# Attention decode on one core: the final wait moved behind the closing barrier, first loads ahead of the opening branch, last head scaled on VectorE

## The chip, the cores and the metric

The kernel runs on one core of one Trainium2 chip. The metric is device microseconds of that core, lower is better. "Span" below is the time from the first to the last instruction that the profiler recorded; it is shorter than the device time.

## The reference, cut to what matters

```python
B, H, Sq, Sk, D = 1, 16, 1, 8192, 256           # bf16
scores = einsum("bhqd,bhkd->bhqk", q, k) * D**-0.5
p = softmax(scores, axis=-1)
return einsum("bhqk,bhkd->bhqd", p, v)
```

One query row per head meets 8192 keys and values. K and V are 67 MB each and every byte is used once, so this is mainly a matter of loading 134 MB.

## The kernel before

The kernel records all operations of each engine in a plan, resolves semaphores, and then emits the plan into one block with a body per engine. In the program the block opens with a branch of each engine to its own body and closes with a branch to a common end, where a barrier of all five engines stands: each engine drains and reports ("gather"), GpSimd collects the reports and lets all go ("release"). An opening barrier of the same kind, which guards some constants (four memsets of GpSimd, 0.236 to 0.425 us; release at 0.597), stands ahead of the block.

Loads of K and V go out on SyncE, 2 MB each (some of V in smaller parts, the last two of 256 KB), four buffers of each kind:

```python
plan.op("act", lambda e: e.dma_start(q16[:, :], q[0, :, 0, :]), "q", dma=(s_q, 16))
for kind, h, x in items:                 # k and v halves in order of use
    ...
        plan.op("sp", lambda e, ...: e.dma_start(b[:, at*D:(at+wd)*D], cols(t, h, c+at, c+at+wd)),
                f"{kind}{n}.{i}", waits, dma=(s, used[id(s)]))
```

VectorE computes three quarters of the scores and TensorE the rest; TensorE multiplies the exponentials with V; ScalarE scales each head's sum by the reciprocal of its denominator:

```python
def final(h):
    s = sl(h)
    act(lambda e: e.activation(out=o[0:1, h*D:(h+1)*D], in_=acc[s][0:1, 0:D],
                               func=ACT.Copy, scale=recip[0:1, s:s+1]),
        f"fin{h}", [f"vfree{2*h+1}", f"rc{h}"], ksem("fin", h))
```

The end, on ScalarE's queue; the first 15 heads have been sent out earlier as "out0":

```python
final(H - 1)
plan.op("act", lambda e: e.dma_start(out[0, H-1, 0:1, :], o[0:1, (H-1)*D:H*D]),
        "out1", [f"fin{H-1}"], dma=(s_o[1], 16))
plan.op("act", lambda e: e.nop(), None, ["out0", "out1"])   # wait for both landings
...
with nc.Block() as block:
    ...                                   # plan.emit for each engine
```

## Time and profile before

| what | value | where it is read |
|---|---|---|
| device time | 323.13 us, median of 6 (322.97 to 323.22) | the timed runs |
| span | 321.3 us, so 1.8 us of the device time lie outside it | first line of the page |
| DMA engines busy | over 90% in 38 of 40 slices, 418 GB/s | slice rows of the page and its DMA line |
| first K load issued | 0.72 us | timeline |
| last matmuls, scaling, output's issue | 317.31, 319.26, 319.75 us | timeline |

Lines of the profile page. In the slice rows, each digit is the busy share of one fortieth of the span in tenths; the group line has count, then busy us and mean ns of one, then the idle time before and its releaser.

```profile
span 321.3 us, 6420 instructions
...
PE 221.4 (69%) x2166; PEld 155.5 (48%) x2166; DVE 275.2 (86%) x1586; ACT 94.1 (29%) x185; POOL 1.9 (1%) x12
DMA  7999999999999999999999999999999999999994
q1 hardware_dynamic: 10080, 134.22, 98.5%
L618 ACT ACTIVATE o<-acc,recip 1x256 bf16<-1x256 f32 x16 | 7.5, 466 | 74.1 <-PE acc L604 74.1
```

The load queue holds the DMA engines for 98.5% of the span: the kernel is one load stream with a head and a tail that nothing covers. The opening, in the timeline (start us, length us, engine, line, operation):

```profile
0.72 0.85 SPq L318 DMA_DIRECT2D Kb<-in_k_dram  x2
0.73 0.40 ACTq L300 DMA_DIRECT2D q<-in_q_dram  x1
```

The end, in the chain of waits (start us, length us, what) and then in the timeline:

```profile
304.67 12.60 DMA Vb<-in_v_dram
317.27 0.04 issue
317.31 1.92 PE acc L604 x16
319.24 0.02 issue
319.26 0.47 ACT o L618
```

```profile
319.26 0.47 ACT L618 ACTIVATE o<-acc,recip 1x256 bf16<-1x256 f32 x1 [7.36 <-PE acc L604]
319.75 0.24 ACTq L686 DMA_DIRECT2D out_dram<-o  x1
```

The timeline leaves semaphore instructions out. They are in the trace's records, and the last 1.3 us consist of them (start us, length us, engine, record; the words at the end are added):

```
319.754 0.238 Scalar  DMA_DIRECT2D     issue of out1
320.857 0.017 Scalar  EVENT_SEMAPHORE  out1's landing is seen
320.912 0.038 Scalar  COMPARE_BRANCH   closing branch; it carries the wait for out0
321.077 0.008 Scalar  DRAIN            ScalarE reports to the closing barrier
321.118 0.017 GpSimd  EVENT_SEMAPHORE  all have reported
321.196 0.017 GpSimd  EVENT_SEMAPHORE  release
321.238 0.017 Sync    EVENT_SEMAPHORE  released
321.242 0.017 Scalar  EVENT_SEMAPHORE  released
321.249 0.021 Vector  EVENT_SEMAPHORE  released
321.249 0.051 Tensor  EVENT_SEMAPHORE  released: end of the span, 321.300
```

From the landing to the end of the span 321.300 - 320.857 = 0.44 us pass with branch, drain and barrier.

### The profile page before, as it was taken

To read this page: it belongs to the slowest core of one execution; us is meant where nothing else is said; L and a number is where in the kernel's file an instruction comes from. 1 tells how busy PE (TensorE), PEld (TensorE's weight loads), DVE (VectorE), ACT (ScalarE), POOL (GpSimd) and SP (SyncE) were. 2 spreads that over 40 slices of the span, in tenths; PEclk is the share of its full clock that TensorE was granted. 3 is DMA by queue.
4 is the path that set the end of the run, shared out by engine and by line. 5 is a ranking of instruction groups with operands and counts; after the bars stand their busy time and mean duration, and the time that the engine had idled before them with its cause. 6 is when DMAs were issued, how large, how long until landed. Compare 5 with 4: busy or idle time off the path is not lost.

```text
span 321.3 us, 6420 instructions
## 1 busy us (share of the span) xinstructions
PE 221.4 (69%) x2166; PEld 155.5 (48%) x2166; DVE 275.2 (86%) x1586; ACT 94.1 (29%) x185; POOL 1.9 (1%) x12
## 2 busy tenths in 40 slices
PE   1645238687676858785977666687567876486896
PEld 0524126565454635563655454455444645354574
DVE  0899999999999999999998988889988889888600
ACT  3453222414233242422141242213322213232010
POOL 2000000000000000000000000000000000000000
PEclk9999999979797987997697898959898779779799
DMA  7999999999999999999999999999999999999994
GB/s 306 434 430 423 428 426 426 426 434 422 425 430 426 430 428 428 430 426 428 430 428 426 428 430 428 426 428 430 427 426 428 430 425 428 432 426 428 416 417 171
DMA packets 10126, 134.36 MB, mean 418 GB/s; under 512 B 1138, under 2 KB 1155, under 8 KB 1796
## 3 DMA queue, kind: packets, MB, share of 16 engines
q1 hardware_dynamic: 10080, 134.22, 98.5%
q8 instruction: 5, 0.08, 0.1%
q14 instruction: 5, 0.04, 0.0%
q10 hardware_dynamic: 36, 0.02, 0.0%
HBM read 134.23 MB, written 0.01 MB: 418 GB/s over the span
## 4 chain that ended last, share of the span: by engine, by line
DVE 46%; DMA 46%; PE 4%; issue 2%; SPq 0%; DVEq 0%; ACT 0%
DVE prod L359 44%; DMA Vb<-in_v_dram 25%; DMA Kb<-in_k_dram 21%; PE acc L604 4%; DVE S L359 2%; DVE g L331 0%; SPq L318 0%; DVE recip L340 0%; DVEq L150 0%; DVE m L378 0%; ACT o L618 0%; DVEq L147 0%; DVEq L144 0%
## 5 line engine op out<-in xcount | busy, mean ns | idle before, releaser
L359 DVE CUSTOM_DVE_ANT_0 prod<-Kb,qbc 128x256 bf16<-128x256 bf16 x768 | 269.1, 411 | 27.2 <-DMA Kb<-in_k_dram 24.7
L604 PE MATMUL acc<-Vb,E 128*1 128x256 bf16 x1024 | 146.0, 312 | 9.8 <-DMA Vb<-in_v_dram 9.8
L604 PEld LDWEIGHTS acc<-Vb,E 128*1 128x1 bf16 x1024 | 95.4, 95 | 52.7 <-DMA Vb<-in_v_dram 11.0
L499 ACT ACTIVATE KT<-tp 128x1024 bf16<-128x1024 bf16 x64 | 62.0, 1021 | 113.1 <-PE tp L490 113.1
L359 DVE DVE_READ_ACCUMULATOR2_ANT S<- 128x1 f32 x768 | 56.7, 74 | 0.0
L490 PE MATMUL tp<-identb,Kb 128*128 128x128 bf16 x512 | 39.0, 237 | 6.0 <-DMA Kb<-in_k_dram 6.0
L490 PEld LDWEIGHTS tp<-identb,Kb 128*128 128x128 bf16 x512 | 33.1, 107 | 14.4 <-issue 10.1
L516 PE MATMUL spe<-qcur,KT 128*128 128x1 bf16 x512 | 20.6, 165 | 19.6 <-ACT KT L499 19.6
L555 PE MATMUL misc<-g,ones_row 1*128 1x1 f32 x32 | 7.0, 286 | 33.7 <-DVE g L331 33.7
L618 ACT ACTIVATE o<-acc,recip 1x256 bf16<-1x256 f32 x16 | 7.5, 466 | 74.1 <-PE acc L604 74.1
L516 PEld LDWEIGHTS spe<-qcur,KT 128*128 128x128 bf16 x512 | 16.4, 98 | 24.5 <-ACT KT L499 24.3
L555 PEld LDWEIGHTS misc<-g,ones_row 1*128 1x128 f32 x32 | 5.7, 220 | 36.8 <-DVE g L331 36.6
L544 PE MATMUL misc<-ident,m 128*1 128x128 f32 x34 | 7.3, 301 | 19.0 <-DVE m L378 19.0
L544 PEld LDWEIGHTS misc<-ident,m 128*1 128x1 f32 x34 | 2.0, 82 | 22.2 <-DVE m L378 21.6
L562 ACT ACTIVATE negb<-misc 128x1 f32<-128x1 f32 x16 | 2.7, 171 | 24.5 <-PE misc L555 24.5
L331 DVE TENSOR_REDUCE g<-misc 1x1 f32<-1x128 f32 x17 | 4.7, 274 | 5.0 <-PE misc L544 5.0
L584 PE MATMUL misc<-ones_col,lsum 128*1 128x1 f32 x34 | 3.2, 164 | 4.1 <-ACT E L569 3.7
L569 ACT ACTIVATE E<-S,negb 128x64 bf16<-128x64 f32 x16 | 5.6, 348 | 0.7 <-ACT negb L562 0.2
L340 DVE RECIPROCAL recip<-misc 1x1 f32<-1x1 f32 x17 | 2.6, 151 | 3.7 <-PE misc L584 3.7
L438 ACT ACTIVATE qbc<-qb 128x256 bf16<-128x256 bf16 x14 | 5.6, 400 | 0.0
L529 ACT ACTIVATE S<-spe 128x16 f32<-128x16 f32 x16 | 3.0, 185 | 7.2 <-PE spe L516 7.2
L412 PE MATMUL tp<-q,identb 16*128 16x256 bf16 x15 | 4.1, 406 | 1.0 <-ACT qb L421 0.5
(25 smaller groups left out, 21.8 us busy)
## 6 DMA issues: line engine op xcount, KB each, us to landing
Kb<-in_k_dram SPq DMA_DIRECT2D x32, 2048.0 KB, 24.3
Vb<-in_v_dram SPq DMA_DIRECT2D x29, 2048.0 KB, 30.3
Vb<-in_v_dram SPq DMA_DIRECT2D x4, 1024.0 KB, 20.4
Vb<-in_v_dram SPq DMA_DIRECT2D x3, 512.0 KB, 11.8
Vb<-in_v_dram SPq DMA_DIRECT2D x2, 256.0 KB, 12.8
q<-in_q_dram ACTq DMA_DIRECT2D x1, 8.0 KB, 3.7
out_dram<-o ACTq DMA_DIRECT2D x1, 7.5 KB
out_dram<-o ACTq DMA_DIRECT2D x1, 0.5 KB
```

Of the source, the lines that this page charges most:

```text
L331: lambda e: e.tensor_reduce(g[0:1, s : s + 1], misc[s][0:1, MT0 : MT0 + P], AX.X, ALU.max),
L359: lambda e, slot=slot, c=c, col=col, h=h, r=(ttr - 1) % PROD: e.tensor_tensor_reduce(out=prod[:, r * D : (r + 1) * D], in0=Kb[slot][:, c * ...
L412: lambda e, i=i, src=src: e.matmul(bank[:, i * D : (i + 1) * D], lhsT=src[0], rhs=src[1], start=True, stop=True),
L438: lambda e: e.activation(out=qbc[:, s * D : (s + 1) * D], in_=qb[:, (h - 2) * D : (h - 1) * D], func=ACT.Copy),
L490: lambda e, c=c, hf=hf, i=(b * NH + hf) * P, view=view: e.transpose(view[:, i : i + P], Kb[slot][:, c * D + hf * P : c * D + (hf + 1) * P] ...
L499: lambda e, gn=gn, view=view: e.activation(out=KT[gn % KT_SLOTS][:, :], in_=view[:, 0 : GROUP * D], func=ACT.Copy),
L516: lambda e, b=b, hf=hf, oc=oc, gn=gn: e.matmul(spe[sl(h)][:, oc : oc + 1], lhsT=KT[gn % KT_SLOTS][:, (b * NH + hf) * P : (b * NH + hf + 1) ...
L544: lambda e: e.matmul(misc[s][0:1, MT0 : MT0 + P], lhsT=m[:, s : s + 1], rhs=ident[:, :], start=True, stop=True),
L555: lambda e: e.matmul(misc[s][:, BC0 : BC0 + 1], lhsT=ones_row[0:1, :], rhs=g[0:1, s : s + 1], start=True, stop=True),
L569: lambda e: e.activation(out=E[:, s * J : (s + 1) * J], in_=S[:, s * J : (s + 1) * J], func=ACT.Exp, bias=negb[:, h : h + 1], scale=SCALE, ...
L604: lambda e, c=c, col=col: e.matmul(a[0:1, 0:D], lhsT=E[:, col : col + 1], rhs=Vb[slot][:, c * D : (c + 1) * D], start=(x == 0 and c == 0), ...
L618: lambda e: e.activation(out=o[0:1, h * D : (h + 1) * D], in_=acc[s][0:1, 0:D], func=ACT.Copy, scale=recip[0:1, s : s + 1],),
```

## The change

The intent: let the closing branch, drain and barrier run while the last output is still in flight; issue the first loads one branch earlier; and scale the last head on an engine that is idle by then. The diff, cut to its core:

```diff
+    def emit_front(self, e, eng, n):
+        for i in range(n):
+            assert not self.ops[e][i][2]
+            self.run(e, eng, i)
+        self.front[e] = n
+
     def emit(self, e, eng, nc=None):
 ...
-        i = 0
+        i = self.front.get(e, 0)
 ...
         def final(h):
             s = sl(h)
+            if h == H - 1:
+                dve(
+                    lambda e: e.tensor_scalar(
+                        o[0:1, h * D : (h + 1) * D], acc[s][0:1, 0:D], recip[0:1, s : s + 1], None, ALU.mult
+                    ),
+                    f"fin{h}",
+                    [f"vfree{2 * h + 1}", f"rc{h}"],
+                )
+                return
 ...
-        plan.op("act", lambda e: e.nop(), None, ["out0", "out1"])
-
         plan.ahead["dve"] = 32
         plan.resolve(sems, alias)
+
+        plan.emit_front("sp", nc.sync, K_SLOTS)
+        plan.emit_front("act", nc.scalar, 1)
 
         with nc.Block() as block:
 ...
+        for s, n in (plan.dma["out0"], plan.dma["out1"]):
+            nc.scalar.wait_ge(s, n)
```

The first loads move ahead of the opening branch, not ahead of the opening barrier.

More of the change, by code (lines that the diff above doesn't have):

```diff
@@ L42, in __init__ @@
         self.ahead = {}
+        self.front = {}
     def op(self, eng, fn, name=None, waits=(), dma=None, sem=None):
```

## The prediction

> **What bounds the kernel now.** The transfers do. The profile page's slice rows show the 16 DMA engines over 90% busy in 38 of 40 slices, and the loads' queue holds them 98.5% of the span at 418 GB/s. VectorE is 86% busy, TensorE 69%. So the 321.3 us span is one load stream with an exposed head (until the first K load is issued) and an exposed tail (after the last V load lands). The change touches these two ends only.
>
> **Head.** In the timeline and its records, SyncE's wait in the opening barrier ends at 0.656 us and the first K load is issued at 0.721. Between lie the opening branch and nothing else: 0.065 us. [...] With the four K loads and the q load ahead of the branch, the first issue should move to about 0.66 to 0.68. The stream is saturated, so the whole of it shifts: 0.05 us gained (estimate).
>
> **Last head's scaling.** The chain ends with the last 16 PV matmuls (1.92 us), then the ScalarE scaling at 319.26, lasting 0.465 (all sixteen are alike), then the output's issue at 319.754. VectorE instead: its reduction of 128 PSUM elements takes 0.274, its reciprocal of one element 0.151, so 256 elements cost about 0.41 (estimate: 0.151 + 256/128 x 0.13, from these two). [...] ScalarE then waits for VectorE's semaphore rather than its own, which I take as nearly free. Gain 0.05 us, all on the chain.
>
> **Tail.** The records of ScalarE after the last issue: landing seen at 320.857, closing branch 320.912, drain 321.077, the barrier's gather on GpSimd 321.118, its release 321.196, all engines released 321.24 to 321.30. So 0.44 us of branch, drain and barrier run after the landing. Afterwards they run while the output flies: issue to landing is 1.10 us, branch to last release 0.39, so they hide fully. What remains after the landing is one or two semaphore waits, about 0.07 us. Gain 0.37 us.
>
> **Sum.** 0.05 + 0.05 + 0.37 = 0.47 us of 323.15: predicted 322.65, span about 320.8. It is 0.15%. The three runs before spread 0.22. Range 322.3 to 323.0. Chances: faster by over 2% 0.005, within 2% 0.985, slower by over 2% 0.01.
>
> **What the profile would show.** (a) First K issue near 0.67 us instead of 0.721. (b) A VectorE tensor_scalar of 1x256 at the end lasting 0.38 to 0.44 us, the output's issue 0.43 to 0.46 us after the last matmul instead of 0.49. (c) The span ends with ScalarE's wait, within 0.1 us of the output's landing, and the other engines' barrier is over about 0.5 us before. (d) DMA share, GB/s and the steady stage unchanged.
>
> **What would make it wrong.** The stream's own scatter (0.2 us) could swallow or double the gain. VectorE's scaling could be slower than estimated, or its semaphore reach ScalarE later, turning 0.05 into a loss. Time outside the span (323.1 measured against 321.3 profiled, 1.8 us) might depend on when engines other than ScalarE finish: if the slowest of them set it, more would be gained; if work after the kernel must follow ScalarE, nothing more.

That the branch takes the 0.065 us, and that the last waits take 0.07 us, are my estimates; the wait records of the two barriers in the kernel before last 0.017 to 0.051 us.

## The result, and the profile after

The changed kernel takes 322.38 us (median of 6 runs, 322.25 to 322.46) against 323.13 us: 0.75 us less. The ratio of the means is 0.9977, 95% interval 0.9964 to 0.999. Here and below a ratio is the mean time of one kernel's runs over that of the other kernel's runs of the same rounds, so it is not quite the ratio of the medians quoted. By the 2% rule the two are the same; the difference is nevertheless clear, because no run of one falls among the runs of the other.

The page:

```profile
span 320.8 us, 6419 instructions
DMA  7999999999999999999999999999999999999995
q1 hardware_dynamic: 10080, 134.22, 98.7%
L635 ACT ACTIVATE o<-acc,recip 1x256 bf16<-1x256 f32 x15 | 7.0, 466 | 60.7 <-PE acc L612 60.7
L627 DVE TENSOR_SCALAR o<-acc,recip 1x256 bf16<-1x256 f32 x1 | 0.5, 471 | 7.5 <-PE acc L612 7.5
```

The steady stage is the same. VectorE's scaling took 471 ns against 466 on ScalarE. The opening, in the timeline:

```profile
0.72 0.85 SPq L326 DMA_DIRECT2D Kb<-in_k_dram  x2
0.73 0.40 ACTq L308 DMA_DIRECT2D q<-in_q_dram  x1
```

Nothing moved: in the records the first K load is issued at 0.722 us, before it was 0.721. The chain of waits at the end, and the timeline:

```profile
304.72 12.42 DMA Vb<-in_v_dram
317.14 0.04 issue
317.19 1.92 PE acc L612 x16
319.11 0.03 issue
319.13 0.47 DVE o L627
```

```profile
319.13 0.47 DVE L627 TENSOR_SCALAR o<-acc,recip 1x256 bf16<-1x256 f32 x1 [7.45 <-PE acc L612]
319.63 0.23 ACTq L703 DMA_DIRECT2D out_dram<-o  x1
```

The records of the last microsecond:

```
319.635 0.233 Scalar  DMA_DIRECT2D     issue of out1
319.909 0.235 Scalar  DRAIN            ScalarE reports to the closing barrier
320.175 0.017 GpSimd  EVENT_SEMAPHORE  all have reported
320.254 0.017 GpSimd  EVENT_SEMAPHORE  release
320.295 0.017 Sync    EVENT_SEMAPHORE  released
320.300 0.017 Scalar  EVENT_SEMAPHORE  released
320.307 0.021 Vector  EVENT_SEMAPHORE  released
320.308 0.051 Tensor  EVENT_SEMAPHORE  released: barrier over at 320.359
320.733 0.038 Scalar  EVENT_SEMAPHORE  out1's landing is seen: end of the span, 320.771
```

The span fell from 321.300 to 320.771, by 0.53 us. Of that, 0.405 us is what followed the landing (0.443 before, 0.038 now). The rest, 0.12 us, lies ahead of the tail: the last matmuls, which wait for the load stream, began at 317.19 in place of 317.31. Yet the device time of these two profiled runs fell by 323.10 - 322.25 = 0.85 us. So device time minus span fell too, from 1.80 to 1.48 us. That part is invisible in the profile. The experiments ask where it comes from, and which part of the change did what.

### The profile page after: what moved, and what is told of

Read it like the earlier page. It is cut to its first block, busy times and chain, and to the rows that moved or that the text cites. A ratio compares the mean times of both kernels' runs of the same rounds, so it can differ in the third digit from the quotient of the medians.

```text
span 320.8 us, 6419 instructions
## 1 busy us (share of the span) xinstructions
PE 221.7 (69%) x2166; PEld 155.1 (48%) x2166; DVE 275.7 (86%) x1587; ACT 93.6 (29%) x184; POOL 1.9 (1%) x12
## 4 chain that ended last, share of the span: by engine, by line
DVE 49%; DMA 45%; PE 2%; issue 2%; SPq 0%; DVEq 0%
DVE prod L367 46%; DMA Kb<-in_k_dram 30%; DMA Vb<-in_v_dram 15%; PE acc L612 2%; DVE S L367 2%; DVE g L339 0%; SPq L326 0%; DVE recip L348 0%; DVE m L386 0%; DVEq L158 0%; DVE o L627 0%; DVEq L155 0%; DVEq L152 0%
## 5 line engine op out<-in xcount | busy, mean ns | idle before, releaser
L498 PE MATMUL tp<-identb,Kb 128*128 128x128 bf16 x512 | 38.2, 234 | 5.0 <-DMA Kb<-in_k_dram 5.0
L498 PEld LDWEIGHTS tp<-identb,Kb 128*128 128x128 bf16 x512 | 32.3, 105 | 13.0 <-issue 10.6
```

What stands on the lines that cost most here:

```text
L498: lambda e, c=c, hf=hf, i=(b * NH + hf) * P, view=view: e.transpose(view[:, i : i + P], Kb[slot][:, c * D + hf * P : c * D + (hf + 1) * P] ...
```

## The experiments

Eleven kernels ran, all with correct results, each with five timed runs against the kernel before on the same chip. The kernel before had a median of 323.06 us in the first two groups of four runs, and of 323.19 us in the group with the last three (wait_dve, early1, early1_sp_act). The groups ran on different chips, so kernels of different groups are compared by their ratios and by their distance from the kernel before. "Outside" is device time minus span, as the median of the five runs (their spans are listed to 0.1 us); for the kernel before it lay between 1.75 and 1.93 us in all 27 runs beside these experiments. It covers whatever lies ahead of the first record as well as what follows the last one.

| kernel | median us (range) | ratio to before [95%] | outside, us |
|---|---|---|---|
| the change | 322.38 (322.25 to 322.46) | 0.9977 [0.9964, 0.9990] | 1.49 |
| tail_only | 322.43 (322.22 to 322.77) | 0.9983 [0.9969, 0.9996] | 1.50 |
| front_only | 323.06 (323.01 to 323.79) | 1.0006 [0.9993, 1.0020] | 1.81 |
| vec_only | 323.05 (322.94 to 323.46) | 1.0002 [0.9989, 1.0016] | 1.77 |
| own_wait | 322.94 (322.88 to 323.44) | 1.0002 [0.9988, 1.0015] | 1.88 |
| wait_sp | 322.28 (322.10 to 322.44) | 0.9975 [0.9962, 0.9989] | 1.42 |
| wait_dve | 322.32 (322.31 to 322.35) | 0.9972 [0.9958, 0.9985] | 1.45 |
| wait_pe | 322.61 (322.32 to 322.77) | 0.9984 [0.9971, 0.9998] | 1.61 |
| wait_pool | 322.74 (322.70 to 322.81) | 0.9990 [0.9976, 1.0004] | 1.84 |
| wait_all | 322.64 (322.62 to 322.81) | 0.9988 [0.9974, 1.0001] | 1.86 |
| early1 | 321.68 (321.54 to 321.77) | 0.9952 [0.9938, 0.9965] | 1.47 |
| early1_sp_act | 321.57 (321.53 to 321.75) | 0.9949 [0.9936, 0.9963] | 1.47 |

### One part at a time

**tail_only**: the kernel before with the wait behind the barrier and nothing else.

```diff
-        plan.op("act", lambda e: e.nop(), None, ["out0", "out1"])
 ...
+        for s, n in (plan.dma["out0"], plan.dma["out1"]):
+            nc.scalar.wait_ge(s, n)
```

> Only the wait is moved behind the closing barrier. Main theory (the tail is the whole gain, and part of it lies outside the profiled span because some engine other than ScalarE needs longer after its last instruction): 322.3 to 322.5 us, 0.6 to 0.8 below before; profiled span 320.9 to 321.0; time minus span 1.45 to 1.55 instead of 1.8. Rival 1 (the shift of time minus span comes from the loads in front of the branch): 322.7, time minus span still 1.8. Rival 2 (half of the gain is a steadier load stream, not the tail): 322.7 with the last V landing where it was.

Measured: 322.43 us, 0.63 below the kernel before in the same rounds, and outside 1.50 us. Its profiled end is that of the change: landing seen at 320.729, end of the span at 320.767. The tail alone gives, within the scatter, the whole gain, the invisible part included. Rival 1 falls: there were no loads ahead of the branch, and the outside time shrank all the same. In this profile too the last matmuls began early, at 317.18 us. They did so in own_wait below as well (317.19), which keeps the old end and is no faster (ratio 1.0002). So the early landing is scatter and not the gain, and rival 2 falls.

**front_only**: the kernel before with the loads ahead of the branch (the `emit_front` lines of the diff).

> Only the first loads stand ahead of the opening branch. Main theory (the branch that is written costs nothing where it carries no wait): the first K load is issued at 0.72 us as before, 323.1 us, within 0.1 of before. As predicted blind: issue at 0.66 to 0.68 and 0.05 us gained. Rival 1 (time outside the span is saved at the start): 322.8, time minus span 1.5.

Measured: 323.06 us, as before, outside 1.81 us. The opening in the timeline:

```profile
0.72 0.41 ACTq L308 DMA_DIRECT2D q<-in_q_dram  x1
0.72 0.85 SPq L326 DMA_DIRECT2D Kb<-in_k_dram  x2
```

The issue did not move (0.723 us in the records). The 0.065 us between the barrier and the first load was not the branch's: with the branch behind the load 0.065 us remain in the change (0.657 to 0.722) and 0.068 here (0.655 to 0.723).

**vec_only**: the kernel before with the `if h == H - 1: dve(...)` of the diff and nothing else.

> Only the last head is scaled on VectorE. Main theory: 0.471 us against ScalarE's 0.465, the output's issue 0.49 to 0.51 us after the scaling starts in both, so 323.1 us, within 0.1 of before. As predicted blind: 0.05 us gained.

Measured: 323.05 us, as before. The instructions that write the output (count, then ns min/median/max):

```profile
L627 ACT ACTIVATE o<-acc,recip x15: 464/464/466, 61.6 to 311.6; 1x256 bf16<-1x256 f32 x15
L619 DVE TENSOR_SCALAR o<-acc,recip x1: 473/473/473, 319.2 to 319.2; 1x256 bf16<-1x256 f32 x1
```

VectorE needed 9 ns more than ScalarE. From the scaling's start to the output's issue it is 0.505 us here (319.218 to 319.723) and 0.496 before (319.258 to 319.754).

**own_wait**: the wait stays ahead of the barrier, but on an instruction of its own, so that the closing branch is a plain one.

```diff
-        plan.op("act", lambda e: e.nop(), None, ["out0", "out1"])
+        s_x = sem("s_x")
+        plan.op("act", lambda e: e.sem_inc(s_x, 1), None, ["out0", "out1"])
```

> Before, with the wait for the output's landing on a semaphore instruction of its own, still ahead of the closing barrier, so that the closing branch carries no wait. Theory (a branch that carries a wait becomes a real compare-and-branch, one that carries none costs nothing): no compare-and-branch on ScalarE at the end; from the landing seen to the end of the span 0.31 to 0.36 us instead of 0.44; time 0.1 us below before, 323.0. Rival (the branch costs the same either way): 0.44 us again, 323.13.

Measured, in the records of ScalarE:

```
319.637 0.238 Scalar  DMA_DIRECT2D     issue of out1
319.915 0.832 Scalar  EVENT_SEMAPHORE  waits for both outputs, until 320.747
320.823 0.008 Scalar  DRAIN            ScalarE reports
```

There is no compare-and-branch any more, and from the end of the wait to the drain 0.076 us pass (320.823 - 320.747) where it was 0.203 (321.077 - 320.874). From the end of the wait to the end of the span it is 0.30 us (321.046 - 320.747); before, 0.43 (321.300 - 320.874). So the branch that carried a wait cost 0.13 us. This rests on one profile of own_wait; with the wait on the branch, front_only and vec_only show 0.42 us, like the kernel before. The branch that carries no wait left no record, and no time that can be told apart: on ScalarE 0.041 us pass from the end of out1's issue to the next record over such a branch (the change, 319.868 to 319.909), and 0.040 with no branch between (own_wait, 319.875 to 319.915). In device time it is not resolved: the median is 0.12 us lower, but two of five runs were slower and the ratio is 1.0002.

### Where the time outside the span comes from

These four, and wait_dve below, are the changed kernel with one line different, the engine that waits behind the barrier:

```diff
-            nc.scalar.wait_ge(s, n)
+            nc.sync.wait_ge(s, n)          # wait_sp; nc.tensor in wait_pe,
+                                           # nc.gpsimd in wait_pool, nc.vector in wait_dve
```

and in wait_all each of the five engines waits. Their theory A: each engine needs its own time after its last recorded instruction, and the device time ends with the engine that is done last.

> The changed kernel with the wait behind the barrier on SyncE in place of ScalarE. Theory A (each engine needs its own time after its last instruction, ScalarE's about 1.5 us, the slowest engine's 1.8 or more): time minus span tells SyncE's; anything from 1.45 (then it is not the slowest) to 1.8 (then it is). Rival B (time minus span is 1.5 whenever the engines leave staggered, whichever comes last): 1.5 here and for TensorE. Sum of both: 322.3 to 322.7 us.

> The same with the wait on TensorE. Theory A, with TensorE as the slowest (its semaphore instruction takes 0.051 us against 0.017 elsewhere): time minus span 1.7 to 1.85, 322.65 us. Rival B: 1.5, 322.38.

> The same with the wait on GpSimd. Theory A: time minus span between 1.45 and 1.8, of no slowest engine if TensorE shows 1.8. Rival B: 1.5, 322.38 us.

> All five engines wait for the landing behind the barrier, so that they leave together as in before. Theory A: time minus span 1.75 to 1.85, 322.65 us: the 0.3 us outside the span is given back and the 0.4 us inside it stays. Rival (the time outside the span does not depend on who leaves when): 1.5, 322.38 us.

> The changed kernel with the wait on VectorE, to fill the row of engines: time minus span was 1.42 for SyncE, 1.49 for ScalarE, 1.61 for TensorE, 1.84 for GpSimd. If each engine has its own time after its last instruction, VectorE shows its own, anywhere from 1.4 to 1.85, with a scatter below 0.1; 322.3 to 322.75 us.

Measured, outside: SyncE 1.42, VectorE 1.45, ScalarE 1.49 (the change), TensorE 1.61, GpSimd 1.84, all five 1.86 us. The spans of the profiled runs are 320.7 to 320.9 in all of them. So theory A holds in form: the time outside the span depends on which engine leaves last, and it is back at the old value as soon as GpSimd is among the last to leave. My guess of the engine was wrong: TensorE is not the slowest, GpSimd is. TensorE's long barrier record (0.051 us, against 0.017 to 0.021 on the others) was no guide. Rival B, that any engine leaving last gives 1.5, falls with wait_pool (no run of it under 1.81).

The numbers also fit together. In the profiled run of wait_pool, the device time is 1.85 us more than the end of GpSimd's last record (320.877); in the kernel before it is 1.89 more (323.10 against 321.213), in wait_all 1.95 (322.62 against 320.667), in own_wait 1.98 (322.94 against 320.959). In wait_sp GpSimd's last record ends at 320.337; 320.337 + 1.85 = 322.19 us, or 322.32 with 1.98 (estimates from these runs), and 322.22 was measured. So in wait_sp GpSimd, released by the barrier 0.48 us earlier, may already be what ends last, and SyncE's own time is at most 1.42 us. The same sum for the change gives 320.271 + 1.85 to 1.98 = 322.12 to 322.25 us, and 322.25 was measured: there too GpSimd may be what ends last. SyncE, VectorE and ScalarE are therefore not told apart; only TensorE (1.57 to 1.72 in its five runs) and GpSimd (1.81 to 1.90) stand out. In the kernel before, all engines are let go at nearly the same time (GpSimd's release at 321.196, the others at 321.238 to 321.249), and the sums fit GpSimd as the one that sets the end. What the engines do after their last record is in no trace, so why GpSimd needs longer stays open.

### Ahead of the barrier, and a version that beats both

If the branch cost nothing, the head can only be shortened by passing the opening barrier. The first K load and the q load need nothing that this barrier guards. **early1** is the changed kernel with these two instructions placed in the first block ahead of the barrier; the other three K loads stay behind it, so that issuing them does not delay SyncE's report to the barrier (the issues of the first four took SyncE 0.37 to 0.74 us each in the kernel before).

```diff
+        first = nc.main_func.blocks[0]
+        n0 = len(first.instructions)
         plan.emit_front("sp", nc.sync, K_SLOTS)
         plan.emit_front("act", nc.scalar, 1)
+        ins = list(first.instructions)
+        at = next(i for i, x in enumerate(ins) if type(x).__name__ == "InstDrain")
+        new = [x for x in ins[n0:] if type(x).__name__ == "InstDMACopy"]
+        move = [new[0], new[-1]]                       # first K load, q load
+        rest = [x for x in ins[n0:] if all(x is not y for y in move)]
+        first.instructions = ins[:at] + move + ins[at:n0] + rest
```

> The changed kernel with the first K load and the q load ahead of the opening barrier, not only of the branch. Theory (the load stream is saturated and starts at its first issue, so the whole kernel shifts with it): first K issue at 0.0 to 0.15 us instead of 0.72, 321.7 to 321.9 us, 0.55 to 0.7 below the changed kernel; last V load ends near 317.3 instead of 317.96. Rival (what the runtime still does at the start, or the small fetches seen before the span, delays the early load; or SyncE's issue delays the barrier and so the work behind it): less than 0.3 us gained.

Measured: 321.68 us, ratio 0.9952. The chain of waits at its start, to be held against "0.72 8.16" in the kernel before and "0.72 7.97" in the change:

```profile
0.00 8.15 DMA Kb<-in_k_dram
8.15 0.03 issue
```

For the kernel before the same lines of the chain are:

```profile
0.72 8.16 DMA Kb<-in_k_dram
8.88 0.03 issue
```

The load is issued at 0.00 and lands 0.73 us earlier than in the kernel before, 0.54 earlier than in the change (8.15 against 8.69). The last packet of the V loads ends at 317.36 us, against 318.07 before and 317.96 in the change. So the stream shifted by 0.60 us against the change at its end, and by 0.71 against the kernel before. In device time the nearest comparison is wait_dve, the change with the wait on VectorE, in the same rounds on the same chip: 322.32 - 321.68 = 0.64 us. The opening barrier's release came 0.20 us later (0.801 against 0.598 us in the change's records) and held nothing up that mattered: the first matmul, which waits for q, still began earlier (4.43 us against 4.53).

**early1_sp_act** adds the wait on SyncE and puts the last scaling back on ScalarE.

> The parts that earned something, together: wait behind the barrier, on SyncE; first K load and q load ahead of the opening barrier; the last head back on ScalarE. Theory: early1 less 0.1 us at most, 321.6 to 321.8 us, since GpSimd, about 1.87 us after its own last instruction, then ends as late as SyncE; time minus span 1.40 to 1.45. Rival (the gains at the two ends exclude each other): no faster than 322.3.

Measured: 321.57 us, ratio 0.9949, outside 1.47 us, above the 1.40 to 1.45 that was expected. With 1.47 for SyncE here and for ScalarE in early1, the choice between these two shows no gain. The two early versions are not told apart from each other (ranges and intervals overlap), as the theory of GpSimd ending about as late would have it. Both beat the kernel before by about 1.5 us and every other version; early1 is 1.51 us below the kernel before of its rounds (323.19 - 321.68), the change was 0.75 below it in its own.

## Why the prediction was right, and where its sum was not

The measured 322.38 us lies in the stated range, 322.3 to 323.0, near its lower edge; the predicted gain was 0.47 us, the measured one 0.75. That the sum stayed inside the range is partly luck: two terms of 0.05 us each were worth nothing, a term of about 0.3 was missing, and the range was 0.7 us wide. The largest term was right in its mechanism. Point by point:

- **The bound.** Right. The stream is untouched by the change, and early1 shows directly that what happens at its head shifts everything: 0.72 us earlier at the first issue, 0.60 us earlier at the last load than in the change.
- **"Head", 0.05 us.** Wrong; it measured nothing. Three openings agree: first issue at 0.721 before, 0.722 with the change, 0.723 in front_only. I took the 0.065 us between the barrier and the load for the branch; that a branch takes about that long was my estimate, and no trace showed it. The records held a warning that I passed over: VectorE needs 0.095 us between two neighbouring instructions with no branch in between (0.743 and 0.838 us, start to start), as much as over its opening branch (0.650 to 0.743).
- **"Last head's scaling", 0.05 us.** Wrong; it measured 0.00 within 0.01. The term that was mis-sized is VectorE's scaling: estimated 0.41, measured 0.471. The estimate mixed a fixed part from a reciprocal with a slope from a reduction, two other operations. That ScalarE sees VectorE's semaphore about as quickly as its own was right: 0.032 us from the end of the scaling to the issue, against 0.030.
- **"Tail", 0.37 us.** Right in mechanism and close in size: 0.405 us inside the span. It left 0.038 us behind the landing where 0.07 was allowed, since both waits went into one instruction. The barrier was over 0.41 us before the end of the span.
- **What was missing.** The sum held the tail's gain to what the profile shows. Another 0.3 us lies outside the span: the engines other than ScalarE are let go earlier, and among them GpSimd: the device time is 1.85 to 1.98 us more than the end of its last record where it is among the last to leave, and 1.49 us more than the span with ScalarE last. The prediction named this as something that could make it wrong ("if the slowest of them set it, more would be gained"), and gave it no number; wait_pool and wait_all show that the end depends on GpSimd.
- **The sum of what was measured.** 0.405 inside and about 0.31 outside (1.80 - 1.49) make 0.72 us, against 0.75 for the change and 0.63 for tail_only. The 0.12 us by which the load stream was shorter in the profiled run of the change is not claimed for it: that stream shows in the spans of the kernel before as a scatter of 321.0 to 321.7 us.

## What to carry to other kernels

In this kernel the wait for the last output cost what stood behind it, 0.443 us with branch, drain and barrier and 0.038 us with nothing but the wait itself. So let the drains and the barrier run while the output flies (1.10 us from its issue to its landing seen, before and after), and, as far as this kernel shows, let an engine other than GpSimd be the last to leave (1.84 us outside the span with it, 1.42 to 1.61 with the others). When a change works at the very end, compare device time with span as well: a gain can lie where the profile has no records (here about 0.31 of 0.75 us). A gap of a plausible length between two records is not yet the cost of the instruction that stands in it (here 0.065 us with the branch in it and 0.065 without); where the load stream is the bound, it is worth asking what the first load really has to wait for (issued 0.72 us earlier in early1, it brought 0.64 us against wait_dve).
